# A fused attention and two-layer-block kernel on one core: four tiles together through block 1, and attention 1.5 pairs ahead

## The chip, the cores and the metric

The kernel runs on one core of one Trainium2 chip. The metric is the device time of one execution in microseconds (us). Lower is better. TensorE is called PE here, VectorE DVE, ScalarE ACT, GpSimd POOL, and SP is the queue that issues most DMAs.

## The reference

```python
# attention: q (1, 12288, 128), kv (1, 384, 32, 128), pooled 4 x 4 -> 768 keys
kv_flat = kv_pool.reshape(B, -1, C) @ w_sr          # k = v = kv_flat
s = scale * (q @ k.transpose(0, 2, 1))
a = np.exp(s - s.max(-1, keepdims=True)); a /= a.sum(-1, keepdims=True) + 1e-09
x = a @ v                                           # (12288, 128)
# block 1 (w_in, w_out: 128 x 2048, 2048 x 128)
h = x @ w_in;  g = h * (1.0 / (1.0 + np.exp(-1.702 * h)));  x = g @ w_out
# block 2, weights of its own
h = x @ w_in;  g = h * np.clip(h + 3.0, 0.0, 6.0) / 6.0;    return g @ w_out
```

All inputs are fp32, except that the weights of both blocks are float64 and must be turned into fp32 pairs on the chip.

## The kernel before

**Tiles and units.** The 12288 rows are 24 tiles `t` of 512. Every product is made of three fp32r matmuls: an operand is split into a high part (a copy on ACT, `act_hi`, L118) and a low part (the difference, on DVE, `dve_lo`, L121), and high times low, high times high and low times high are added up in PSUM. A block is cut into eight units per tile, `(m, t, j)`, each of 256 columns of the hidden layer. A unit's first half is `unit_mm` (six matmuls of 512 columns into the PSUM tile `h`, which has two buffers), then the activation, the split of its result into `gh` (ACT) and `gl` (DVE), and `unit_out` (six matmuls of 512 columns into `acc`). In block 1 the activation is a gelu on ACT (L347); in block 2 a relu on ACT (L351) and `unit_swish`, one pass on DVE (L355).

**The main loop** runs over steps `s` (L491). Step `s` issues `unit_mm(s)`, then `unit_out(s - 3)`, then whatever a table `beside` has for (step, "mm"); after that the list `ORDER[m]` gives the order in which ACT's, DVE's and POOL's work of the step is issued. Every engine takes its instructions strictly in that order. Before, the units run by pairs of tiles: 16 steps of block 1, then 16 steps of block 2, so 32 steps a pair and 384 in all.

**Attention beside it.** For each tile there are four subtiles `i`. `s_mm` (L209) makes scores, `s_max` (DVE), `s_exp` (ACT, with the sums as a side output) and `s_norm` (two tiny DVE operations and a scaling on POOL, L234) follow. `t_mm` (L242) transposes the exponentials on PE, `t_hi` and `t_lo` split them. `av_mm` (L267, 18 matmuls, in two halves) multiplies by the values, and `av_end` splits the result into the block's input `x1`. Scores and transposes in the loop share one PSUM tile, `st`, that has a single buffer: the next user must wait until the exp, or `t_lo`, of the last one has read it. `plan_scores` and `plan_values` put these into `beside` by the step numbers in `S_STEPS`, `T_STEPS` and `AV_STEPS`; before, a pair's 32 steps hold the values of the next pair and the scores of the pair after that.

**Weights.** A block's weights are 8 pieces of 512 columns, 16 in all. `w_bits` (six DVE operations) turns the words of a float64 piece into fp32 parts, `w_hi` (ACT) and `w_lo` (two DVE operations) split them. Six pieces are converted in the loop over `kv` ahead of everything (`W_EARLY`), the other ten beside the steps of `W_STEPS`.

**Ahead of the main loop** stand the pooling of `kv` (L446) and a list `FIRST` of pieces for the attention of tiles 0 to 3: `S`core, `T`ranspose, `A` (values), `Q` (split of q), `v`, `W` (a conversion's end), with the stages of each piece issued by `FIRST_STAGES` (stage, how many pieces later).

Of the kernel before, what the change touches and what calls it, by code (L numbers as in the profile page):

```python
# [11 lines left out]
F32 = mybir.dt.float32  # L12
# [6 lines left out]
P = 128  # L19
# [8 lines left out]

T_STEPS = (0, 2, 4, 6, 10, 12, 13, 15)
T_STEPS_0 = (3, 4, 5, 6, 10, 12, 13, 15)
AV_STEPS = (8, 17)
S_STEPS = (16, 18, 20, 22, 24, 26, 28, 30)

ORDER = {
    1: "t_hi gelu w_hi hi_last hi max exp t_lo lo_last lo rest norm end w_lo w_bits".split(),
    2: "max t_hi t_lo relu swish w_hi hi_last exp lo_last norm end rest w_lo w_bits".split(),
}


FIRST = (
    "W S00 S01 S02 S03 v T00 S10 T01 S11 T02 S12 T03 S13 Q2 A0 T10 S20 T11 S21 T12 S22 T13 Q3 "
    "S23 S30 S31 S32 S33"
).split()

FIRST_STAGES = (
    ("t_hi", 0), ("max", 0), ("exp", 1), ("av_end", 0), ("norm", 2), ("w_lo", 0), ("t_lo", 0),
)
A1_STEP = 1  # L50


W_LOADS = {0: "g", 2: "g", 4: "g", 6: "r", 8: "r", 10: "ws"}
W_EARLY = (1, 3, 5, 7, 9, 11)
W_PLACES = "- - - r r ws r r ws r r ws - - ws -".split()
W_STEPS = (0, 2, 3, 5, 7, 9, 11, 13, 16, 18)
POOL_LO = (19, 22)


UPPER_MIN = float(np.uint32(896 << 20).view(np.float32))  # L60
# [4 lines left out]
def tile_pooled_attention__moe_gelu__moe_hardswish(  # L65
# [45 lines left out]
    def f(ap):  # L111
        return ap.bitcast(F32)
# [38 lines left out]
    def w_load(tag):  # L151
        w, src, cs = w_todo.pop(0)
        s = work.tile([P, WL, 2], U32, tag=tag, name="ws", bufs={"g": 3, "r": 2, "ws": 1}[tag])
        nc.sync.dma_start(out=s, in_=src[:, cs, :])
        w_ready.append((w, s, cs))

    def w_bits():

        w, ws, cs = w_ready.pop(0)
        upper = ws[:, :, 1]
        a = work.tile([P, WL], U32, tag="o", name="wa")
        b = work.tile([P, WL], U32, tag="wb", name="wb")
        nc.vector.tensor_scalar(
            out=a, in0=upper, scalar1=0x7FFFFFFF, scalar2=None, op0=ALU.bitwise_and
        )
        nc.vector.tensor_scalar(
            out=f(a), in0=f(a), scalar1=UPPER_MIN, scalar2=UPPER_MAX, op0=ALU.max, op1=ALU.min
        )  # L170
        nc.vector.tensor_scalar(
            out=b, in0=a, scalar1=3, scalar2=0x3FFFFFFF,
            op0=ALU.logical_shift_left, op1=ALU.bitwise_and,
        )
        nc.vector.scalar_tensor_tensor(  # L175
            out=a, in0=upper, scalar=0xC0000000, in1=b, op0=ALU.bitwise_and, op1=ALU.bitwise_or
        )
        nc.vector.tensor_scalar(
            out=b, in0=a, scalar1=0xFF800000, scalar2=None, op0=ALU.bitwise_and
        )  # L180
        nc.vector.scalar_tensor_tensor(
            out=f(b), in0=ws[:, :, 0], scalar=2.0 ** -52, in1=f(b), op0=ALU.mult, op1=ALU.mult
        )
        w_half.append((w, cs, a, b))
        place = w_places.pop(0)
        if place != "-":
            w_load(place)

    def w_hi():
        w, cs, a, _ = w_half[0]  # L190
        act_hi(w[0][:, cs], f(a))

    def w_lo():

        w, cs, a, c = w_half.pop(0)
        dve_lo(f(a), f(a), w[0][:, cs])
        nc.vector.tensor_tensor(out=w[1][:, cs], in0=f(a), in1=f(c), op=ALU.add)

# [22 lines left out]
    def s_exp(t, i):  # L221
        ps, nm = ps_s.pop((t, i)), e_t[t, i]
        e = e_t[t, i] = work.tile([P, NK], F32, tag="e", name="e", bufs=8)
        z = sums_t[t, i] = tiny.tile([P, 1], F32, tag="sums", name="sums")
        nc.scalar.activation(
            e.rearrange("p (b k) -> p b k", b=2), ps[:, :, :h], AF.Exp, bias=nm, accum_out=z
        )

    def s_norm(t, i):
        e, z = e_t[t, i], sums_t.pop((t, i))  # L230
        rec = tiny.tile([P, 1], F32, tag="rec", name="rec")
        nc.vector.tensor_scalar(out=rec, in0=z, scalar1=EPS, scalar2=None, op0=ALU.add)
        nc.vector.reciprocal(out=rec, in_=rec)
        nc.gpsimd.tensor_scalar(  # L234
            out=e, in0=e, scalar1=rec, scalar2=1.0, op0=ALU.mult, op1=ALU.mult
        )

    def t_mm(t, i, *tag):
        e = e_t.pop((t, i))
# [32 lines left out]
    def av_end(t):  # L272
        x1[t] = split_acc(av_acc.pop(t), "x1")

    def split_acc(acc, tag):
        hi = work.tile([P, TT], F32R, tag=tag + "h", name=tag + "h")
        lo = work.tile([P, TT], F32R, tag=tag + "l", name=tag + "l")
        act_hi(hi, acc)
        dve_lo(lo, acc, hi)
        return hi, lo  # L280


    units = []
    for k in range(0, NT, 2):
        for m in (1, 2):
            for t in (k, k + 1):
                units += [(m, t, j) for j in range(NU)]


# [9 lines left out]
    def plan_scores(t, steps):  # L299
        at(steps[0] - 3, "rest", split_q, t)  # L300
        for i, step in enumerate(steps):
            at(step, "mm", s_mm, t, i)
            at(step + 1, "max", s_max, t, i)
            at(step + 1, "exp", s_exp, t, i)
            at(step + 1, "norm", s_norm, t, i)

    def plan_values(t, t_steps, av_step):
        for i, step in enumerate(t_steps):
            at(step, "mm", t_mm, t, i)
            at(step + 1, "t_hi", t_hi, t, i)  # L310
            at(step + 1, "t_lo", t_lo, t, i)
        for k in range(2):
            at(av_step + k, "mm", av_mm, t, range(k * KC // 2, (k + 1) * KC // 2))
        at(av_step + 1, "rest", av_end, t)

    for k in range(2, NT, 2):
        s0 = 2 * (k - 2) * NU
        ts = [s0 + x for x in (T_STEPS_0 if k == 2 else T_STEPS)]
        plan_values(k, ts[:SUB], s0 + AV_STEPS[0])
        plan_values(k + 1, ts[SUB:], s0 + AV_STEPS[1])  # L320
        if k + 2 < NT:
            ss = [s0 + x for x in S_STEPS]
            plan_scores(k + 2, ss[:SUB])
            plan_scores(k + 3, ss[SUB:])
    for s in W_STEPS:
        at(s, "w_bits", w_bits)
        at(s + 1, "w_hi", w_hi)
        at(s + 1, "w_lo", w_lo)
    for k in range(2):
        at(A1_STEP + k, "mm", av_mm, 1, range(k * KC // 2, (k + 1) * KC // 2))  # L330
    at(A1_STEP + 1, "rest", av_end, 1)

    h_t, r_t, g_t, gs_t, acc_t = {}, {}, {}, {}, {}

# [29 lines left out]

    def unit_lo(u):
        gh, gl = gs_t[u]
        (pool_lo if u in POOL_LO else dve_lo)(gl, g_t.pop(u), gh)

    def unit_out(u):
        m, t, j = units[u]  # L370
# [11 lines left out]
    def unit_end(u):  # L382
        m, t, j = units[u]
        if j < NU - 1:
            return
        acc = acc_t.pop((m, t))
        if m == 1:
            x2[t] = split_acc(acc, "x2")
        else:
            o = work.tile([P, TT], F32, tag="o", name="o")  # L390
            nc.scalar.activation(o, acc, AF.Copy, scale=1.0 / 6.0)
            nc.sync.dma_start(out=outT[:, t * TT:(t + 1) * TT], in_=o)

    with tc.manual_schedule():
# [38 lines left out]
        for g_ in range(n_g):  # L433
            pk = big(*slots[g_])[:, 0, :kg]
            cs = slice(g_ * kg, (g_ + 1) * kg)
            for w_ in range(n_w):
                i = g_ * n_w + w_
                if i in (4, 10):
                    split_q(i // 10)
                if i in W_EARLY:  # L440
                    w_bits()
                    w_hi()
                    if i < W_EARLY[-1]:
                        w_lo()
                for w in range(kw // kg):
                    nc.tensor.matmul(  # L446
                        pk, wsr_sb, kvs[i][:, w * kg:(w + 1) * kg],
                        start=(w_ == 0 and w == 0), stop=(w_ == n_w - 1 and w == kw // kg - 1),
                    )
                if w_ == 3 and g_ > 0:  # L450
                    v_group(g_ - 1)
            nc.scalar.activation(k_h[:, cs], pk, AF.Copy, scale=scale / (R * R))
            nc.vector.scalar_tensor_tensor(
                out=k_l[:, cs], in0=pk, scalar=scale / (R * R), in1=f(k_h[:, cs]),
                op0=ALU.mult, op1=ALU.subtract,
            )
            kf[g_] = work.tile([P, kg], F32, tag="x2" + "hhl"[g_], name="kf")
            nc.scalar.activation(kf[g_], pk, AF.Copy, scale=1.0 / (R * R))


        def piece(kind, t=0, i=0):
# [2 lines left out]
                slots.append(slots.pop(0))  # L464
            if kind == "S":
                s_mm(t, i, *slots[-1])
                return {"max": (s_max, t, i), "exp": (s_exp, t, i), "norm": (s_norm, t, i)}
            if kind == "T":
                t_mm(t, i, *slots[-1])
                return {"t_hi": (t_hi, t, i), "t_lo": (t_lo, t, i)}  # L470
# [1 line left out]
                av_mm(t, range(KC))  # L472
                return {"av_end": (av_end, t)}
            if kind == "W":
                return {"w_lo": (w_lo,)}
            if kind == "Q":
                split_q(t)
            else:
# [10 lines left out]

        nu = len(units)  # L490
        for s in range(nu + LAG):  # L491
            if s < nu:
                unit_mm(s)
            if s >= LAG:
# [59 lines left out]
```

## Time and profile before

| | |
|---|---|
| median of 3 runs | 1394.12 us (1393.7 to 1396.24) |
| the profiled execution, its own time | 1396.09 us |
| its span, first to last instruction | 1394.3 us |
| PE busy | 1353.2 us (97%), 6294 matmuls |
| DVE busy | 986.3 us (71%) |
| ACT busy | 1012.3 us (73%) |
| POOL busy | 129.5 us (9%) |
| mean granted clock of PE | 0.990 |

The profiled execution's time is 1.8 us above its span, and 2.0 us above the median. Busy shares are means over the whole span; the page also has the span in 40 slices, where PE shows 7, 8, 6, 8, 8, 9, 9 tenths in the first seven slices (34.9 us each) and 9 or more in all that follow but the last.

### The profile page before, as it was taken

What the parts mean: (1) busy time and instruction counts of PE and PEld (TensorE: products, weight loads), DVE (VectorE), ACT (ScalarE), POOL (GpSimd) and SP (SyncE); (2) the same over time, 40 slices, a digit from 0 to 9 for tenths busy, and PEclk for the clock granted to TensorE, in tenths of its full rate; (3) what the DMA queues carried; (4) which work ended last, traced back from release to release, by engine and by line L of the source; (5) the groups of instructions that cost most, each with busy time, mean ns of one, the idle gap of its engine ahead of it and who ended that gap; (6) DMA issues with size and microseconds to landing.
All of it is one profiled execution on the core that took longest, in us unless ns stands there. A gap on an engine that the chain in (4) does not pass through costs nothing.

```text
span 1394.3 us, 16502 instructions
## 1 busy us (share of the span) xinstructions
PE 1353.2 (97%) x6294; PEld 1132.9 (81%) x6294; DVE 986.3 (71%) x1140; ACT 1012.3 (73%) x1199; POOL 129.5 (9%) x128
## 2 busy tenths in 40 slices
PE   7868899999999999999999999999999999999998
PEld 5756788888888888888888888888888888888887
DVE  7678995686587577478578568568568658757667
ACT  2556678778678678768768777777877877866776
POOL 1310030010010010011011011001001001000000
PEclk9989999999999999999999999999999999999999
DMA  8011000000000000000000000000000000000000
GB/s 326 24 53 46 24 16 8 8 16 8 9 16 8 8 8 16 8 9 16 0 8 16 8 8 16 8 8 16 8 8 16 9 8 8 8 1 8 8 1 16
DMA packets 11167, 28.38 MB, mean 20 GB/s; under 512 B 1232, under 2 KB 1360, under 8 KB 11088
## 3 DMA queue, kind: packets, MB, share of 16 engines
q1 hardware_dynamic: 10944, 27.27, 5.6%
q8 instruction: 49, 0.80, 0.2%
q14 instruction: 30, 0.25, 0.1%
q10 hardware_dynamic: 144, 0.07, 0.0%
HBM read 21.04 MB, written 6.29 MB: 20 GB/s over the span
## 4 chain that ended last, share of the span: by engine, by line
PE 91%; DVE 5%; ACT 2%; issue 1%; DMA 0%; POOL 0%; ACTq 0%; POOLq 0%; DVEq 0%
PE h L343 12%; PE h L342 12%; PE h L341 12%; PE acc L380 12%; PE acc L378 12%; PE acc L379 12%; PE acc L267 6%; PE st L209 6%; PE st L242 4%; PE h L446 1%; DVE gl L121 1%; DVE wa L175 1%; DVE nm L216 1%; ACT gh L118 1%; PE h L209 1%
## 5 line engine op out<-in xcount | busy, mean ns | idle before, releaser
L121 DVE TENSOR_TENSOR gl<-g,gh 128x1024 fp32r<-128x1024 f32 x382 | 472.1, 1238 | 270.4 <-ACT gh L118 270.3
L118 ACT ACTIVATE gh<-g 128x1024 fp32r<-128x1024 f32 x384 | 404.9, 1057 | 26.7 <-PE acc L379 24.0
L351 ACT ACTIVATE r<-h 128x1024 f32<-128x1024 f32 x192 | 197.4, 1028 | 181.6 <-PE h L343 181.6
L380 PE MATMUL acc<-gl,wo_h 128*128 128x512 f32 x768 | 300.2, 391 | 0.4 <-DVE gl L121 0.4
L378 PE MATMUL acc<-gh,wo_l 128*128 128x512 f32 x768 | 300.1, 391 | 0.0
L379 PE MATMUL acc<-gh,wo_h 128*128 128x512 f32 x768 | 299.7, 390 | 0.0
L355 DVE SCALAR_TENSOR_TENSOR g<-r,h 128x1024 f32<-128x1024 f32 x192 | 234.1, 1219 | 91.9 <-ACT r L351 86.2
L347 ACT ACTIVATE g<-h 128x1024 f32<-128x1024 f32 x192 | 197.0, 1026 | 79.1 <-PE h L343 79.0
L380 PEld LDWEIGHTS acc<-gl,wo_h 128*128 128x128 f32 x768 | 144.4, 188 | 32.0 <-DVE gl L121 0.8
L379 PEld LDWEIGHTS acc<-gh,wo_h 128*128 128x128 f32 x768 | 144.5, 188 | 31.9
L378 PEld LDWEIGHTS acc<-gh,wo_l 128*128 128x128 f32 x768 | 144.6, 188 | 30.9
L341 PE MATMUL h<-x1h,wi_l 128*128 128x512 f32 x384 | 158.3, 412 | 0.0
L343 PE MATMUL h<-x1l,wi_h 128*128 128x512 f32 x384 | 151.4, 394 | 0.0
L342 PE MATMUL h<-x1h,wi_h 128*128 128x512 f32 x384 | 151.0, 393 | 0.0
L341 PE MATMUL h<-x2h,wi_l 128*128 128x512 f32 x384 | 150.5, 392 | 0.4 <-DVE g L355 0.4
L343 PE MATMUL h<-x2l,wi_h 128*128 128x512 f32 x384 | 150.8, 393 | 0.0
L342 PE MATMUL h<-x2h,wi_h 128*128 128x512 f32 x384 | 150.4, 392 | 0.0
L234 POOL TENSOR_SCALAR e<-e,rec 128x768 f32<-128x768 f32 x96 | 87.9, 917 | 576.2 <-ACT r L351 246.5
L242 PE MATMUL st<-ident,e 128*128 128x128 f32 x540 | 75.6, 277 | 19.2 <-DVE eTl L121 18.5
L242 PEld LDWEIGHTS st<-ident,e 128*128 128x128 f32 x540 | 65.0, 142 | 32.4 <-issue 11.7
L121 DVE TENSOR_TENSOR eTl<-st,eTh 128x768 fp32r<-128x768 f32 x90 | 85.7, 952 | 1.0 <-ACT eTh L118 0.9
L343 PEld LDWEIGHTS h<-x1l,wi_h 128*128 128x128 f32 x384 | 72.7, 189 | 16.1
(79 smaller groups left out, 1440.9 us busy)
## 6 DMA issues: line engine op xcount, KB each, us to landing
kvs<-kvT SPq DMA_DIRECT2D x12, 512.0 KB, 9.7
q_f<-qT SPq DMA_DIRECT2D x24, 256.0 KB, 2.6
outT<-o SPq DMA_DIRECT2D x24, 256.0 KB, 2.0
ws<-w_in SPq DMA_DIRECT2D x8, 512.0 KB, 4.6
ws<-w_out SPq DMA_DIRECT2D x8, 512.0 KB, 3.8
wsr_sb<-w_sr ACTq DMA_DIRECT2D x1, 64.0 KB, 4.6
```

What stands on the lines that cost most here:

```text
L118: nc.scalar.activation(hi, x, AF.Copy)
L121: nc.vector.tensor_tensor(out=lo, in0=x, in1=f(hi), op=ALU.subtract)
L242: nc.tensor.transpose(pt[:, c // 4, c % 4 * P:(c % 4 + 1) * P], e[:, c * P:(c + 1) * P], ident)
L341: nc.tensor.matmul(hp[:, c, :], wi[m][1][:, ch], xh, start=True, stop=False)
L342: nc.tensor.matmul(hp[:, c, :], wi[m][0][:, ch], xh, start=False, stop=False)
L343: nc.tensor.matmul(hp[:, c, :], wi[m][0][:, ch], xl, start=False, stop=True)
L347: nc.scalar.activation(g, h_t.pop(u), AF.Gelu_apprx_sigmoid)
L351: nc.scalar.activation(r, h_t[u], AF.Relu, bias=3.0)
L355: nc.vector.scalar_tensor_tensor(out=g, in0=r_t.pop(u), scalar=6.0, in1=h_t.pop(u), op0=ALU.min, op1=ALU.mult)
L378: nc.tensor.matmul(acc, wo[m][1][:, ch], gh[:, c, :], start=first, stop=False)
L379: nc.tensor.matmul(acc, wo[m][0][:, ch], gh[:, c, :], start=False, stop=False)
L380: nc.tensor.matmul(acc, wo[m][0][:, ch], gl[:, c, :], start=False, stop=last)
```

## The change

1. The first four tiles form one group: 32 steps of block 1, then 32 steps of block 2. Pairs follow as before.
2. The ten conversions in the loop stand at steps 0, 3, 6, ..., 27 in place of 0, 2, 3, 5, ..., 18. `w_bits` keeps four DVE operations, `w_lo` gets the other two and so has four, one step later. One conversion of the `kv` loop moves, whole, into `FIRST` behind `Q2`. The loads of weights are issued from `w_lo`.
3. The order of a step changes: in block 1, `t_lo` comes second, and `w_hi` behind `hi`; in block 2 conversions fall out.
4. In the pair of tiles `k` and `k + 1`, values are now made for `k + 1` and `k + 2` (before: `k + 2` and `k + 3`) and scores for `k + 3` and `k + 4` (before: `k + 4` and `k + 5`). Transposes in steps of block 1 are issued ahead of the step's `unit_mm` (place "first"), and split in the same step; those in block 2 stay behind `unit_out` and are split one step later. `T_STEPS` and `AV_STEPS` change, `S_STEPS` keeps its numbers.
5. The normalization of a tile's four subtiles is done at once, after the fourth. Two `gl` of early units go from POOL back to DVE. `x2` of tiles 2 and 3 borrows the buffers of weights.

```diff
-T_STEPS = (0, 2, 4, 6, 10, 12, 13, 15)
-T_STEPS_0 = (3, 4, 5, 6, 10, 12, 13, 15)
-AV_STEPS = (8, 17)
-S_STEPS = (16, 18, 20, 22, 24, 26, 28, 30)
+FOUR = 4
+T_STEPS = (0, 2, 4, 5), (8, 10, 12, 14)
+AV_STEPS = (6, 6), (15, 16)
+S_STEPS = (16, 18, 20, 22), (24, 26, 28, 30)
+T_STEPS_0 = {2: (4, 5, 7, 8), 3: (14, 16, 18, 20), 4: (47, 49, 51, 53)}
+AV_STEPS_0 = {1: (1, 2), 2: (11, 12), 3: (21, 22), 4: (55, 56)}
+S_STEPS_0 = {4: (32, 34, 36, 38), 5: (40, 42, 44, 46), 6: (56, 58, 60, 62)}
-    1: "t_hi gelu w_hi hi_last hi max exp t_lo lo_last lo rest norm end w_lo w_bits".split(),
-    2: "max t_hi t_lo relu swish w_hi hi_last exp lo_last norm end rest w_lo w_bits".split(),
+    1: "t_hi t_lo gelu hi_last hi w_hi lo_last lo rest end w_lo w_bits".split(),
+    2: "max t_hi t_lo relu swish hi_last exp lo_last norm end rest".split(),
-    "W S00 S01 S02 S03 v T00 S10 T01 S11 T02 S12 T03 S13 Q2 A0 T10 S20 T11 S21 T12 S22 T13 Q3 "
+    "S00 S01 S02 S03 v T00 S10 T01 S11 T02 S12 T03 S13 Q2 W A0 T10 S20 T11 S21 T12 S22 T13 Q3 "
-    ("t_hi", 0), ("max", 0), ("exp", 1), ("av_end", 0), ("norm", 2), ("w_lo", 0), ("t_lo", 0),
+    ("t_hi", 0), ("max", 0), ("exp", 1), ("w_hi", 1), ("w_lo", 1), ("av_end", 0), ("norm", 2),
+    ("t_lo", 0), ("w_bits", 0),
-W_EARLY = (1, 3, 5, 7, 9, 11)
-W_STEPS = (0, 2, 3, 5, 7, 9, 11, 13, 16, 18)
-POOL_LO = (19, 22)
+W_EARLY = (1, 3, 5, 7, 9)
+W_STEPS = (0, 3, 6, 9, 12, 15, 18, 21, 24, 27)
...
-    def s_norm(t, i):
+    def s_norm(t, i, n=1):
+        if n == 0:
+            return
+        parts = range(i + 1 - n, i + 1)
...
+        for r, p in enumerate(parts):
+            e = e_t[t, p]
+            nc.gpsimd.tensor_scalar(
+                out=e, in0=e, scalar1=rec[:, r:r + 1], scalar2=1.0, op0=ALU.mult, op1=ALU.mult
+            )
...
-    for k in range(0, NT, 2):
+    for tiles in [range(FOUR)] + [(k, k + 1) for k in range(FOUR, NT, 2)]:
         for m in (1, 2):
-            for t in (k, k + 1):
+            for t in tiles:
                 units += [(m, t, j) for j in range(NU)]
...
+    def plan_values(t, t_steps, av_steps):
         for i, step in enumerate(t_steps):
-            at(step, "mm", t_mm, t, i)
-            at(step + 1, "t_hi", t_hi, t, i)
-            at(step + 1, "t_lo", t_lo, t, i)
...
+            late = units[step][0] == 2
+            at(step, "mm" if late else "first", t_mm, t, i)
+            at(step + late, "t_hi", t_hi, t, i)
+            at(step + late, "t_lo", t_lo, t, i)
...
+    for k in range(FOUR, NT, 2):
+        s0 = 2 * k * NU
+        for i in range(2):
+            if k + 1 + i < NT:
+                plan_values(k + 1 + i, [s0 + x for x in T_STEPS[i]], [s0 + x for x in AV_STEPS[i]])
+            if k + 3 + i < NT:
+                plan_scores(k + 3 + i, [s0 + x for x in S_STEPS[i]])
...
         for s in range(nu + LAG):
+            run(s, "first")
             if s < nu:
                 unit_mm(s)
```

## Rows read from the trace of the kernel before

**Rows 1.** Windows, late stretch: busy us of each engine (instructions), PEclk, DMA share, GB/s
```profile
326.00:382.00 56.00, 56.00 (x270) 46.59 (x269) 32.62 (x31) 42.85 (x47) 1.81 (x1) 1.00 0.03 11
```

**Rows 2.** Timeline of PE, late stretch: start us, us, engine, line, operation, tiles [idle before <-releaser]
```profile
316.09 0.51 PE L209 MATMUL st<-k_h,q_h 128*128 128x384 f32 x2
319.91 0.39 PE L341 MATMUL h<-x1h,wi_l 128*128 128x512 f32 x1
322.64 0.81 PE L242 MATMUL st<-ident,e 128*128 128x128 f32 x6
...
328.79 0.82 PE L242 MATMUL st<-ident,e 128*128 128x128 f32 x6
...
376.97 0.40 PE L341 MATMUL h<-x2h,wi_l 128*128 128x512 f32 x1
```

**Rows 3.** Timeline of PE, steps 0 to 32
```profile
73.10 0.50 PE L341 MATMUL h<-x1h,wi_l 128*128 128x512 f32 x1
...
98.37 1.54 PE L242 MATMUL st<-ident,e 128*128 128x128 f32 x6 [10.61 <-DVE eTl L121]
...
110.58 1.51 PE L242 MATMUL st<-ident,e 128*128 128x128 f32 x6 [2.97 <-DVE eTl L121]
...
142.37 1.51 PE L242 MATMUL st<-ident,e 128*128 128x128 f32 x6 [4.59 <-DVE eTl L121]
...
147.50 0.39 PE L378 MATMUL acc<-gh,wo_l 128*128 128x512 f32 x1
...
172.88 0.62 PE L209 MATMUL st<-k_h,q_h 128*128 128x384 f32 x2 [1.20 <-ACT e L225]
...
210.22 0.39 PE L341 MATMUL h<-x1h,wi_l 128*128 128x512 f32 x1
```

**Rows 4.** Timeline of DVE, steps 0 to 14
```profile
78.94 1.23 DVE L121 TENSOR_TENSOR gl<-g,gh 128x1024 fp32r<-128x1024 f32 x1 [2.91 <-ACT gh L118]
...
88.01 0.42 DVE L165 TENSOR_SCALAR wa<-ws 128x512 uint32<-128x512 uint32 x1
...
90.11 0.43 DVE L178 TENSOR_SCALAR wb<-wa 128x512 uint32<-128x512 uint32 x1
...
91.72 1.22 DVE L121 TENSOR_TENSOR gl<-g,gh 128x1024 fp32r<-128x1024 f32 x1 [0.45 <-ACT gh L118]
92.86 0.69 DVE L121 TENSOR_TENSOR wa<-wa,wo_h 128x512 f32<-128x512 f32 x1
...
94.19 0.42 DVE L165 TENSOR_SCALAR wa<-ws 128x512 uint32<-128x512 uint32 x1
...
97.37 0.95 DVE L121 TENSOR_TENSOR eTl<-st,eTh 128x768 fp32r<-128x768 f32 x1
...
142.14 2.28 DVE L121 TENSOR_TENSOR gl<-g,gh 128x1024 fp32r<-128x1024 f32 x1
```

**Rows 5.** Timeline of ACT, late stretch
```profile
321.45 0.20 ACT L225 ACTIVATION_READ_ACCUMULATOR e<-st,nm 128x1 f32 x1
...
350.85 1.03 ACT L347 ACTIVATE g<-h 128x1024 f32<-128x1024 f32 x1 [2.51 <-PE h L343]
352.04 1.06 ACT L118 ACTIVATE gh<-g 128x1024 fp32r<-128x1024 f32 x1 [0.16 <-PE acc L379]
...
380.56 1.28 ACT L225 ACT_TABLE_LOAD   x1
...
382.66 0.19 ACT L225 ACTIVATION_READ_ACCUMULATOR e<-st,nm 128x1 f32 x1
```

**Rows 6.** Timeline of all engines, 30 to 36 us, and of DVE at 58 us
```profile
30.57 1.63 DVE L197 TENSOR_TENSOR wo_l<-wa,wb 128x512 fp32r<-128x512 f32 x1
...
35.46 0.69 PE L209 MATMUL h<-k_h,q_h 128*128 128x384 f32 x1 [5.63 <-ACT k_h L452]
...
35.64 0.41 DVE L453 SCALAR_TENSOR_TENSOR k_l<-st,k_h 128x256 fp32r<-128x256 f32 x1
...
58.03 0.69 DVE L121 TENSOR_TENSOR x1l<-acc,x1h 128x512 fp32r<-128x512 f32 x1 [3.03 <-ACT x1h L118]
```

More of the change, by code (lines that the diff above doesn't have):

```diff
@@ L47 @@
 FIRST_STAGES = (
-    ("t_hi", 0), ("max", 0), ("exp", 1), ("av_end", 0), ("norm", 2), ("w_lo", 0), ("t_lo", 0),
+    ("t_hi", 0), ("max", 0), ("exp", 1), ("w_hi", 1), ("w_lo", 1), ("av_end", 0), ("norm", 2),
+    ("t_lo", 0), ("w_bits", 0),
 )
-A1_STEP = 1
 W_LOADS = {0: "g", 2: "g", 4: "g", 6: "r", 8: "r", 10: "ws"}
-W_EARLY = (1, 3, 5, 7, 9, 11)
-W_PLACES = "- - - r r ws r r ws r r ws - - ws -".split()
-W_STEPS = (0, 2, 3, 5, 7, 9, 11, 13, 16, 18)
-POOL_LO = (19, 22)
+W_EARLY = (1, 3, 5, 7, 9)
+W_PLACES = "- - - r r ws r r ws r r - r r - -".split()
+W_STEPS = (0, 3, 6, 9, 12, 15, 18, 21, 24, 27)
 UPPER_MIN = float(np.uint32(896 << 20).view(np.float32))
@@ L177, in w_bits, with w_hi, w_lo @@
         )
+        w_half.append((w, ws, cs, a, b))
+    def w_hi():
+        w, _, cs, a, _ = w_half[0]
+        act_hi(w[0][:, cs], f(a))
+    def w_lo():
+        w, ws, cs, a, c = w_half.pop(0)
         nc.vector.tensor_scalar(
-            out=b, in0=a, scalar1=0xFF800000, scalar2=None, op0=ALU.bitwise_and
+            out=c, in0=a, scalar1=0xFF800000, scalar2=None, op0=ALU.bitwise_and
         )
         nc.vector.scalar_tensor_tensor(
-            out=f(b), in0=ws[:, :, 0], scalar=2.0 ** -52, in1=f(b), op0=ALU.mult, op1=ALU.mult
+            out=f(c), in0=ws[:, :, 0], scalar=2.0 ** -52, in1=f(c), op0=ALU.mult, op1=ALU.mult
         )
-        w_half.append((w, cs, a, b))
         place = w_places.pop(0)
@@ L187, in w_bits @@
             w_load(place)
[L189 to L195, printed above, removed]
         dve_lo(f(a), f(a), w[0][:, cs])
@@ L223, in s_exp @@
         e = e_t[t, i] = work.tile([P, NK], F32, tag="e", name="e", bufs=8)
-        z = sums_t[t, i] = tiny.tile([P, 1], F32, tag="sums", name="sums")
+        if i == 0:
+            sums_t[t] = tiny.tile([P, SUB], F32, tag="sums", name="sums")
+        z = sums_t[t][:, i:i + 1]
         nc.scalar.activation(
@@ L227, in s_exp @@
         )
-    def s_norm(t, i):
-        e, z = e_t[t, i], sums_t.pop((t, i))
-        rec = tiny.tile([P, 1], F32, tag="rec", name="rec")
+    def s_norm(t, i, n=1):
+        if n == 0:
+            return
+        parts = range(i + 1 - n, i + 1)
+        z = sums_t[t][:, parts[0]:i + 1]
+        rec = tiny.tile([P, n], F32, tag="rec", name="rec")
         nc.vector.tensor_scalar(out=rec, in0=z, scalar1=EPS, scalar2=None, op0=ALU.add)
         nc.vector.reciprocal(out=rec, in_=rec)
-        nc.gpsimd.tensor_scalar(
-            out=e, in0=e, scalar1=rec, scalar2=1.0, op0=ALU.mult, op1=ALU.mult
-        )
+        for r, p in enumerate(parts):
[3 more added lines that the diff above has]
+            )
     def t_mm(t, i, *tag):
@@ L273, in av_end, with split_acc @@
         x1[t] = split_acc(av_acc.pop(t), "x1")
-    def split_acc(acc, tag):
-        hi = work.tile([P, TT], F32R, tag=tag + "h", name=tag + "h")
-        lo = work.tile([P, TT], F32R, tag=tag + "l", name=tag + "l")
+    def split_acc(acc, tag, place=None):
+        if place == "ws":
+            both = work.tile([P, 2, TT], F32R, tag="ws", name=tag, bufs=1)
+            hi, lo = both[:, 0, :], both[:, 1, :]
+        else:
+            hi, lo = (
+                work.tile([P, TT], F32R, tag=place or tag + s, name=tag + s) for s in "hl"
+            )
         act_hi(hi, acc)
@@ L304, in plan_scores @@
             at(step + 1, "exp", s_exp, t, i)
-            at(step + 1, "norm", s_norm, t, i)
-    def plan_values(t, t_steps, av_step):
+            if i == SUB - 1:
+                at(step + 1, "norm", s_norm, t, i, SUB)
+    def plan_values(t, t_steps, av_steps):
         for i, step in enumerate(t_steps):
-            at(step, "mm", t_mm, t, i)
-            at(step + 1, "t_hi", t_hi, t, i)
-            at(step + 1, "t_lo", t_lo, t, i)
[L312 to L324, printed above, removed]
+            late = units[step][0] == 2
+            at(step, "mm" if late else "first", t_mm, t, i)
+            at(step + late, "t_hi", t_hi, t, i)
+            at(step + late, "t_lo", t_lo, t, i)
+        for k, step in enumerate(av_steps):
+            at(step, "mm", av_mm, t, range(k * KC // 2, (k + 1) * KC // 2))
+        at(av_steps[-1], "rest", av_end, t)
+    for t, steps in AV_STEPS_0.items():
+        plan_values(t, T_STEPS_0.get(t, ()), steps)
+    for t, steps in S_STEPS_0.items():
+        plan_scores(t, steps)
+    for k in range(FOUR, NT, 2):
[5 more added lines that the diff above has]
+                plan_scores(k + 3 + i, [s0 + x for x in S_STEPS[i]])
     for s in W_STEPS:
@@ L328, in tile_pooled_attention__moe_gelu__moe_hardswish @@
         at(s + 1, "w_lo", w_lo)
-    for k in range(2):
-        at(A1_STEP + k, "mm", av_mm, 1, range(k * KC // 2, (k + 1) * KC // 2))
-    at(A1_STEP + 1, "rest", av_end, 1)
     h_t, r_t, g_t, gs_t, acc_t = {}, {}, {}, {}, {}
@@ L366, in unit_lo @@
         gh, gl = gs_t[u]
-        (pool_lo if u in POOL_LO else dve_lo)(gl, g_t.pop(u), gh)
+        dve_lo(gl, g_t.pop(u), gh)
     def unit_out(u):
@@ L387, in unit_end @@
         if m == 1:
-            x2[t] = split_acc(acc, "x2")
+            x2[t] = split_acc(acc, "x2", {2: "ws", 3: "wb"}.get(t))
         else:
@@ L442, in tile_pooled_attention__moe_gelu__moe_hardswish @@
                     w_hi()
-                    if i < W_EARLY[-1]:
-                        w_lo()
+                    w_lo()
                 for w in range(kw // kg):
@@ L466, in piece @@
                 s_mm(t, i, *slots[-1])
-                return {"max": (s_max, t, i), "exp": (s_exp, t, i), "norm": (s_norm, t, i)}
+                return {"max": (s_max, t, i), "exp": (s_exp, t, i), "norm": (s_norm, t, i, 1 if t < 2 else i // 3 * SUB)}
             if kind == "T":
@@ L474, in piece @@
             if kind == "W":
-                return {"w_lo": (w_lo,)}
+                return {"w_bits": (w_bits,), "w_hi": (w_hi,), "w_lo": (w_lo,)}
             if kind == "Q":
```

## The prediction

> **What bounds the kernel now.** I read the windows first. In a late stretch of 56 us PE is busy for all 56, at the full clock, while DVE and ACT have a fifth or more of it free [rows 1]. So nothing can be won there, and any new wait of PE is paid in full. PE's timeline gives the prices of the work: a step of twelve matmuls with nothing beside it takes 319.91 to 322.64 = 2.73 us (0.2275 a matmul); two steps and one transposed subtile take 322.64 to 328.79 = 6.15, so a transpose costs 0.69; scores (316.09 to 319.91, less a step) cost 1.09; the 18 matmuls of a tile's values 18 x 0.2275 = 4.10 [rows 2].
>
> The first 32 steps are another matter. They run from 73.10 to 210.22, 137.1 us [rows 3]. Their PE work is 192 + 174 matmuls of the units (83.3), eight transposes (5.5), three tiles of values (12.3) and eight scores (8.7): 109.8. So 27.3 us are lost, and the rows name what ends the waits: DVE's `eTl`, the low half of the transposed subtile before [rows 3]. After a wait PE also runs at half clock, 1.2 of 2.4 GHz: from 142.37 to 147.50 a transpose takes 1.51 in place of 0.81 [rows 2, 3]. DVE is late because it converts weights. A conversion takes, from DVE's starts, 2.10 for four operations, 1.61 - 0.45 = 1.16 for the next two, 1.33 for the last two: 4.59; a `gl` 1.14, an `eTl` 0.87 to the next start and 0.95 in itself [rows 4].
>
> **Four tiles in block 1.** The 32 steps now hold 32 `gl` (36.5), ten conversions (45.9), eight `eTl` (7.0) and six splits of half a `gl`'s size (some 3.5): 93 us of DVE. Before, they held 16 `swish` of a `gl`'s size and eight maxima of an `eTl`'s size more: 18 + 7 more, so 118. PE's work is 109.8 less the eight scores: 101.1. DVE is no longer the longer sum. What remains is local. Followed by hand from `gl` at 78.94: DVE has `gl` 0, four operations, `gl` 1, four operations of 2.49, `gl` 2, a split, `gl` 3, four operations of the second conversion: 11.85, so `eTl` of tile 2's first subtile runs from 90.8 to 91.75 [rows 4]. Its second transpose now stands first in step 5. PE gets there at 73.10, plus steps 0 to 3 without the first three `unit_out` (10.92 - 4.10), the values of tile 1 (4.10), a transpose (0.69) and step 4 (2.73): 87.45 [rows 2, 3]. PE waits **4.2**, rounding off the gaps. A wait of 2.97 and one of 4.59 were each followed by half clock; the second lasted 5.1 us, which cost 2.6, and for the first I take half of that: **2.0** for this one [rows 3]. The fourth transpose (step 8) follows the third by one step, with the conversion of step 6 between them on DVE. `gl` 6 ends some 4.8 after the start of step 6 (1.36 of matmuls, 1.2 from the gelu's start to the copy's, 1.06 of copy, 1.14 of `gl` [rows 4, 5]); with 2.10 and 0.95 that is 7.85, and PE is there after 2.73 + 0.69 + 2.73 = 6.15: **1.7**. At step 11 the values of tile 2 take the `acc` that `x2` of tile 0 frees; its copy now stands behind `w_hi`, which waits for the conversion: **0.7** by the same count, 0 to 1.5. Tile 3's transposes are two steps apart (6.15, or 8.9 from a conversion) and find `eTl` done. Sum **8.6**, against 27.3 lost before: **-18.7**. Bounds: 6.4 if the clock stays up and the last wait is none; 14 if every wait brings half clock of 2.6 and DVE slips by one conversion's half.
>
> **The transpose that stands first.** This is the price of "1.5 pairs ahead". `st` has one buffer. A pair's last scores are in its step 30, and their exp in step 31, behind relu and copy, which wait for that step's own matmuls. In the late stretch the reading of the sums ends at 321.45 + 0.20 = 321.65 [rows 5], and PE starts the next pair's step 0 at 319.91 [rows 2]. Before, the transpose came after that step's twelve matmuls, at 322.64, when `st` had been free for 1.0. Now it comes at 319.91 and must wait until 321.70 (0.05 allowed for the release): **1.79**, with everything of PE behind it. Nothing before it moves: `S_STEPS` and the order relu, copy, exp stand. It meets the pairs that follow scores in step 30, nine of ten (the last has none), and once more inside the four, where a transpose at step 47 stands behind scores at 46, at the same distance (there after twelve matmuls, 2.73, with the exp 4.5 after the step's start): ten times, **+17.9**. Queued behind the waiting transpose is all of PE; behind its split on ACT stand the table load and the gelu of step 0, now some 1.5 later. They do not make PE late again: gelu and copy take some 2.1 of a step's 2.73 [rows 2, 5], so ACT gains 0.6 a step, and `unit_out` of step 0 is three steps off. The row that speaks for no clock penalty is the wait of 1.20, after which the scores went on at full clock [rows 3]; 2.97 is on the other side. 1.79 is nearer to 1.20. If it fell, each would cost another 1.4 to 2.6.
>
> **The values that move away from step 17.** Before, halves of the values stood in steps 17 and 18; now in 15 and 16. The first exp of a block 2 needs a new function table: load 380.56 to 381.84, sums read at 382.85, 5.88 after step 17's first matmul at 376.97 [rows 2, 5]. The next scores are due two steps after it, 5.46, where the values gave 4.1 more. So **0.45** a time (5.93 - 5.46), nine pairs and once in the four: **+4.5**. Bounds 0 and 5.
>
> The Trainium skill speaks against this place (ScalarE: Activation LUTs, What ACT_TABLE_LOAD costs): a switch is about 1283 ns of load and about 1380 ns of drain. The load agrees with the row; by the page's sum the scores would wait 1.83 in place of 0.45 and the total would be higher by ten times 1.38, 13.8. In the row the exp and the reading of its sums are over 1.01 after the load's end, which leaves no place for such a drain.
>
> **Ahead of the loop.** The sixth conversion leaves the `kv` loop. DVE ended the fifth at 30.57 + 1.63 = 32.2; then ACT's copy of the sixth stood ahead of the copies of `k`, PE waited 5.63 until 35.46, and `k_l` ended at 36.05 [rows 6]. Now `v_l` and `k_l`, about 0.4 each, end at 33.0: 3.1 earlier, and up to 5 if PE then keeps its full clock. Against that the conversion's 4.59 come back between tile 0's values, where DVE had 3.03 idle [rows 6], and can start only after the last reciprocal there: 1.6 to 4.6 lost, 2.4 taken. Net **-1.8**, between +1.5 and -3.4. Fewer reciprocals and one pair of table loads less are off PE's path: nothing.
>
> **Edits at nothing.** Work back to DVE from POOL (two `gl`), POOL's four scalings in a row and the borrowed buffers lie where DVE has 23 us of 56 free [rows 1]. The longest `gl` of the early steps took 2.28 in place of 1.23 [rows 4]; even two like it after each row of scalings, 2.1 us, fit into the three steps (8.2) that lie between a `unit_mm` and its `unit_out`, of which matmuls, ACT and `gl` need 4.8. Should that cover go, it is 2.1 a tile. Loads of weights go out one step later, on SP, but pieces were there steps ahead.
>
> **Sum.** -18.7 + 17.9 + 4.5 - 1.8 = **+1.9** on the profiled execution's 1396.1 (span 1394.3 and 1.8 outside), so 1398.0; the median of the runs lies 2.0 lower, 1394.1, and gives **1396.0**. This kernel's measurement tells some 0.2%, 2.8 us, from no change.
>
> **Rivals.**
> *Clock.* The clock falls at each wait of 1.79. At 1.4 to 2.6 each, ten times: 14 to 26 more, 1410 to 1422. It decides from one half of the ten on. For it: 2.97 was enough; against: 1.20 was not. Chance 0.12.
> *No wait at the pair's start.* Then -18.7 - 1.8 and a part of the 4.5: 1374 to 1378. It would need the exp to come 1.8 earlier; that it waits for step 31's relu speaks against. Chance 0.08.
> *DVE still too long* in the first 28 steps: its 93 against 101.1 leave little, and with each conversion a third late the loss is 14 or more: 1401 to 1405. Chance 0.12.
> *A better start*: ahead of the loop -3.4, the first steps 6.4, no wait for the table: 1388 to 1391. Chance 0.11.
> *The table's drain*, as the page has it: 1409. Chance 0.02.
>
> **From cases to numbers.** My forecast, 0.55, is 1396, in its own range 1391 to 1401; of it I give 0.06 faster, 0.32 same, 0.17 slower. Faster: 0.06 + 0.08 + 0.11, less 0.01 = 0.24. Same: 0.32 + 0.01 + 0.02 from the third = 0.35. Slower: 0.17 + 0.12 + 0.10 + 0.02 = 0.41. The range leaves out the clock rival and the absent wait, 0.20 together: 1385 to 1409.
>
> **What would show it.** Right: PE waits of about 1.6 to 1.8 on ACT's exp at each pair's first transpose, 0.3 to 0.5 on the same at the second scores; in the first steps one wait of some 4 on `eTl`, and none of 10. Wrong: PE busy throughout the late stretch, or PE's clock under 1.00 at the pairs' starts, or waits for `gl`.

## The result, and the profile after

The changed kernel takes 1405.45 us (median of 4 runs, 1404.25 to 1405.79), the kernel before 1394.34 (4 runs): a ratio of 1.0076 with a 95% interval of 1.0058 to 1.0093. It is slower by 11 us. The forecast was 1396, with a range of 1385 to 1409 and the largest of its three chances, 0.41, on slower. The profiled execution's span is 1404.0 us, 9.7 longer than before.

The page's head and slices of the changed kernel:

```profile
span 1404.0 us, 16412 instructions
PE 1354.8 (96%) x6294; PEld 1128.0 (80%) x6294; DVE 973.6 (69%) x1010; ACT 1014.7 (72%) x1199; POOL 134.1 (10%) x126
PE   7789999999999999999999999999999999999998
```

PE's work is the same, 6294 matmuls. The third to fifth slices are fuller than before, and yet the whole is longer, so the loss is too thin to show in tenths. Windows show it. The first one below has the bounds of [rows 1]; it holds none of the long waits, only one of 0.29. The second is as long and holds one of the long waits; the third is the 8 us behind another:

```profile
326.00:382.00 56.00, 55.71 (x260) 46.46 (x259) 36.42 (x35) 41.50 (x49) 3.10 (x2) 1.00 0.03 10
400.00:456.00 56.00, 54.23 (x261) 44.78 (x260) 32.71 (x32) 43.42 (x49) 3.56 (x4) 1.00 0.02 6
521.00:529.00 8.00, 7.86 (x41) 6.71 (x42) 4.08 (x6) 6.37 (x8) 3.56 (x4) 1.00 0.00 0
```

The waits of PE over the whole span say what ends the idle time (us in total, times, longest):

```profile
PE st L253 <- issue: 15.7, 10, 1.7
PE st L253 <- DVE eTl L125: 6.4, 2, 4.6
...
PE h L212 <- DVE eTl L125: 4.4, 2, 4.2
PE st L212 <- ACT e L230: 2.9, 10, 0.3
...
PE st L253 <- ACT e L230: 1.6, 1, 1.6
```

The row of 15.7 holds nine waits of 1.68 in the loop and one of 0.59 ahead of it; the last row is the tenth of the same kind, at 296.44.

PE's timeline places the waits. L253 is the transpose (L242 before), L212 the scores (L209), L358 a unit's first matmul (L341):

```profile
59.90 0.61 PE L212 MATMUL h<-k_h,q_h 128*128 128x384 f32 x2 [4.21 <-DVE eTl L125]
...
73.80 0.40 PE L358 MATMUL h<-x1h,wi_l 128*128 128x512 f32 x1
...
92.93 1.51 PE L253 MATMUL st<-ident,e 128*128 128x128 f32 x6 [4.58 <-DVE eTl L125]
...
98.77 0.39 PE L397 MATMUL acc<-gl,wo_h 128*128 128x512 f32 x1
...
107.06 0.85 PE L253 MATMUL st<-ident,e 128*128 128x128 f32 x6 [1.79 <-DVE eTl L125]
...
119.47 0.96 PE L278 MATMUL acc<-eTh,v_l 128*128 128x512 f32 x3 [0.67 <-DVE x2l L125]
...
185.02 0.39 PE L358 MATMUL h<-x2h,wi_l 128*128 128x512 f32 x1
...
239.78 0.85 PE L253 MATMUL st<-ident,e 128*128 128x128 f32 x6 [1.68 <-issue]
...
476.11 0.62 PE L212 MATMUL st<-k_h,q_h 128*128 128x384 f32 x2 [0.29 <-ACT e L230]
...
521.14 0.84 PE L253 MATMUL st<-ident,e 128*128 128x128 f32 x6 [1.68 <-issue]
...
537.12 0.85 PE L253 MATMUL st<-ident,e 128*128 128x128 f32 x6
```

And ACT's, at the same places (compare [rows 5]):

```profile
473.77 1.28 ACT L230 ACT_TABLE_LOAD   x1
475.06 0.90 ACT L230 ACTIVATE e<-st,nm 128x768 f32<-128x768 f32 x1
475.86 0.19 ACT L230 ACTIVATION_READ_ACCUMULATOR e<-st,nm 128x1 f32 x1
...
520.83 0.20 ACT L230 ACTIVATION_READ_ACCUMULATOR e<-st,nm 128x1 f32 x1
```

The first 32 steps run from 73.80 to 185.02, 111.2 us against 137.1 [rows 3]; eight scores, 8.7, have only moved, so 17.2 are won. The wait of 10.6 is gone. From there on each pair gives something back: its 32 steps, from first matmul to first matmul, take 112.37 in place of 109.7 (319.91 - 210.22 [rows 2, 3]). At 521.14 a pair's first transpose starts 0.11 after the sums were read (520.83 + 0.20); the profile calls this releaser "issue" because ACT was just done, but it is the end of the exp, as the row of 1.6 names it. At 476.11 the second scores of a block start 0.06 after the same event behind the table load. The idle times of 1.68 and 0.29 leave out 0.17 of the matmul before, whose end overlaps the next one in an unbroken stream (0.39 long, 0.23 apart): what PE loses is 1.85 and 0.46.

### The profile page after: what moved, and what is told of

The parts are those of the page before. It is cut to its first block, busy times and chain, and to the rows that moved or that the text cites. A ratio compares the mean times of both kernels' runs of the same rounds, so it can differ in the third digit from the quotient of the medians.

```text
span 1404.0 us, 16412 instructions
## 1 busy us (share of the span) xinstructions
PE 1354.8 (96%) x6294; PEld 1128.0 (80%) x6294; DVE 973.6 (69%) x1010; ACT 1014.7 (72%) x1199; POOL 134.1 (10%) x126
## 4 chain that ended last, share of the span: by engine, by line
PE 88%; DVE 4%; ACT 4%; issue 2%; DMA 0%; POOL 0%; SPq 0%; ACTq 0%; DVEq 0%; POOLq 0%
PE h L360 12%; PE h L359 12%; PE h L358 12%; PE acc L397 12%; PE acc L395 12%; PE acc L396 12%; PE st L212 7%; PE acc L278 6%; PE st L253 4%; ACT e L230 1%; ACT gh L122 1%; ACT r L368 1%; DVE gl L125 1%; ACT L230 1%; DVE wa L178 0%
## 5 line engine op out<-in xcount | busy, mean ns | idle before, releaser
L358 PE MATMUL h<-x1h,wi_l 128*128 128x512 f32 x384 | 157.9, 411 | 0.0
L360 PE MATMUL h<-x2l,wi_h 128*128 128x512 f32 x368 | 144.3, 392 | 0.0
L359 PE MATMUL h<-x2h,wi_h 128*128 128x512 f32 x368 | 144.0, 391 | 0.0
L358 PE MATMUL h<-x2h,wi_l 128*128 128x512 f32 x368 | 143.1, 389 | 0.0
L245 POOL TENSOR_SCALAR e<-e,rec 128x768 f32<-128x768 f32 x96 | 96.5, 1024 | 335.6 <-PE st L253 230.6
L128 POOL TENSOR_TENSOR q_l<-q_f,q_h 128x512 fp32r<-128x512 f32 x24 | 36.9, 1537 | 816.7 <-ACT q_h L122 816.7
L253 PE MATMUL st<-ident,e 128*128 128x128 f32 x540 | 74.8, 275 | 24.5 <-issue 15.7
L253 PEld LDWEIGHTS st<-ident,e 128*128 128x128 f32 x540 | 63.0, 141 | 41.9 <-issue 30.8
```

What stands on the lines that cost most here:

```text
L253: nc.tensor.transpose(pt[:, c // 4, c % 4 * P:(c % 4 + 1) * P], e[:, c * P:(c + 1) * P], ident)
L358: nc.tensor.matmul(hp[:, c, :], wi[m][1][:, ch], xh, start=True, stop=False)
L359: nc.tensor.matmul(hp[:, c, :], wi[m][0][:, ch], xh, start=False, stop=False)
L360: nc.tensor.matmul(hp[:, c, :], wi[m][0][:, ch], xl, start=False, stop=True)
```

## The experiments

All runs are against the changed kernel, 1405.4; the kernel before ran beside them at 1393.9 to 1395.1. A difference of about 1 us says nothing: with the same instructions ahead of it, the loop starts between 72.61 and 74.64 in seven profiles (the changed kernel and runs 1, 2, 3, 5, 7 and 9), and the same first 32 steps take 109.99 to 111.22 in five (the changed kernel and runs 1, 2, 3 and 5). The length of one pair, 112.37, repeats within 0.1, so each effect on the pairs is best read there; it is given for the pair that starts at step 128.

**1. Only the first transpose of a pair back behind `unit_out`.**

```diff
-            late = units[step][0] == 2
+            late = units[step][0] == 2 or step % 32 == 0
```

> Only the first transposed subtile of each later pair (step 0 of the pair) goes back behind unit_out and is split one step later; all else as in the changed kernel, 1405.4 us. Theory A (it stands at the head of the step and waits 1.85 us for st, which ACT's exp of step 31 still reads): nine of the ten waits of 1.68 by the profile go, the one at step 47 of the four stays; 1405.4 - 16.7 = 1388.7, between 1387 and 1391. Theory B (the pair's start waits for the normalized exponentials, because all four scalings of a tile now come at once on POOL): the transpose still waits, less than 4 us gained. Theory C (the loss of a pair is spread over many small waits of the new step order): 3 to 8 us gained.

Measured: 1412.08, ratio to before 1.0134 (1.0109 to 1.016). All three theories missed. The wait on the exp is gone, as A said, but the next transpose, still at the head of step 2, now waits for the low half of the first. Waits of PE from 330 to 1300 us, then PE's row and DVE's, of this run:

```profile
PE st L253 <- DVE eTl L125: 19.0, 8, 2.4
```
```profile
527.73 0.85 PE L253 MATMUL st<-ident,e 128*128 128x128 f32 x6 [2.37 <-DVE eTl L125]
```
```profile
526.63 0.95 DVE L125 TENSOR_TENSOR eTl<-st,eTh 128x768 fp32r<-128x768 f32 x1
```

The split of the first was issued a step later, behind a table load, a gelu and two copies on ACT. So 2.37 stands in place of 1.68, 0.69 more, and a pair takes 112.77, 0.40 more; the other 0.28 comes back at the fourth transpose, as the section on the prediction shows. The rest of the rise of 6.6 is the last pair, which had no such wait and now has one of 1.24, and the clock: after one of the nine waits of 2.3 to 2.4 PE ran at half clock for some 3.4 us. The eight us behind two of them:

```profile
1091.00:1099.00 8.00, 7.39 (x39) 6.32 (x40) 3.87 (x4) 5.91 (x7) 0.28 (x1) 1.00 0.10 36
1204.00:1212.00 8.00, 7.36 (x29) 6.02 (x30) 3.89 (x4) 4.75 (x6) 0.32 (x1) 0.79 0.01 2
```

The wait follows the place at the head of a step, not the one transpose.

**2. ACT's exp directly behind max.**

```diff
-    2: "max t_hi t_lo relu swish hi_last exp lo_last norm end rest".split(),
+    2: "max exp t_hi t_lo relu swish hi_last lo_last norm end rest".split(),
```

> Only ACT's order in a step of block 2 changes: exp directly behind max, ahead of relu and the copy. Nothing of PE's order moves. Theory A: the exp then ends some 2.1 us after its scores, before the next step's end, so the waits of 1.85 at the pairs' starts and at step 47 (ten) and of 0.46 behind the table load (ten) all go: 1405.4 - 23 = 1382.5, between 1380 and 1387; relu comes up to 0.5 us later (2 behind a table load), which the three steps before unit_out should hide. Theory B (scalings on POOL): no change, 1404 to 1406. Rival to A: the later relu makes swish and gl late and PE waits for gl in place of the exp: 1390 to 1405.

Measured: 1485.63, ratio 1.0648 (1.0632 to 1.0664). A's number is off by 100 us, and the rival had the right kind and too small a size. Waits of PE from 330 to 1300 us:

```profile
PE h L358 <- DVE g L372: 40.2, 56, 0.9
PE st L253 <- ACT e L230: 19.4, 8, 2.4
```

ACT's timeline of this run:

```profile
503.49 0.90 ACT L230 ACTIVATE e<-st,nm 128x768 f32<-128x768 f32 x1 [2.81 <-DVE nm L219]
504.29 0.19 ACT L230 ACTIVATION_READ_ACCUMULATOR e<-st,nm 128x1 f32 x1
504.38 1.02 ACT L368 ACTIVATE r<-h 128x1024 f32<-128x1024 f32 x1
```

I had overlooked that the exp waits for DVE's max. In front, it stops ACT for 2.81 us, relu and swish come late, and PE waits for a free `h`, which has two buffers, in 56 steps, seven in each pair's sixteen of block 2. A pair takes 120.16. The waits at the pairs' starts did not go either, so the run says nothing for or against the place of the transposes; it shows that the exp's place behind relu, against one directly behind max, is worth 80 us.

**3. The values of a pair's second tile one step later.**

```diff
-AV_STEPS = (6, 6), (15, 16)
+AV_STEPS = (6, 6), (16, 17)
```

> Only the values of a pair's second tile move back by one step, from steps 15 and 16 to 16 and 17, so that 2.04 us of PE work stand between the table load's step and the second scores. Theory A: the wait of 0.46 at the second scores of nine pairs goes, the one in the four stays: 1405.4 - 4.1 = 1401.3, between 1400.5 and 1402.5. Rival: these waits are covered elsewhere (the time comes back as a longer wait at the pair's start): 1405 to 1406.

Measured: 1399.72, ratio 1.0034 (1.0021 to 1.0047). The nine short waits of the pairs are gone and the long ones unchanged (8 of 1.7 from 330 to 1300 us). The gain is 5.7 where 4.1 was expected. A pair takes 111.85, 0.52 less, so nine pairs give 4.7; the loop of this profile also starts 1.2 earlier, which the edit can't cause. The direction holds, and the rival is out.

**4. Normalization one subtile at a time.**

```diff
-            if i == SUB - 1:
-                at(step + 1, "norm", s_norm, t, i, SUB)
+            at(step + 1, "norm", s_norm, t, i, 1)
...
```

The list ahead of the loop is changed in the same way for tiles 2 and 3.

> Only the normalization goes back to one subtile at a time (two tiny DVE operations and one scaling on POOL for each exp). Theory A: off the path, 1404.5 to 1406.5, and the ten waits at the pairs' starts stay at 1.68 by the profile. Theory B (the scalings in a row on POOL delay the transposes or DVE's gl): 1385 to 1395.

Measured: 1404.30, ratio 1.0065 (1.005 to 1.0081), and PE's waits in the late stretch stay:

```profile
PE st L253 <- ACT e L230: 13.0, 8, 1.6
PE st L212 <- ACT e L230: 2.6, 9, 0.3
```

A pair takes 112.36. The four scalings in a row do not matter; theory B is out. That the releaser is now named ACT's exp also confirms how "issue" was read above.

**5. The whole first set of a pair's transposes behind `unit_out`.** The first three are split one step later, the fourth at the end of its own step, since the values follow at once.

```diff
-            at(step, "mm" if late else "first", t_mm, t, i)
-            at(step + late, "t_hi", t_hi, t, i)
-            at(step + late, "t_lo", t_lo, t, i)
+            behind = step >= 64 and step % 32 in (0, 2, 4, 5)
+            last = behind and step % 32 == 5
+            at(step, "mm" if late or behind else "first", t_mm, t, i)
+            after = step + (late or behind and not last)
+            at(after, "rest" if last else "t_hi", t_hi, t, i)
+            at(after, "rest" if last else "t_lo", t_lo, t, i)
```

> All four transposes of a pair's first tile (steps 0, 2, 4, 5) go behind unit_out, the first three split one step later, the last at the end of its own step; the rest as in the changed kernel, 1405.4 us. The run that moved the first one alone lost its wait on the exp but won nothing, because the second, still at the head of step 2, then waited 2.37 us for the low half of the first. Theory A (a place at the head of a step leaves 2.7 us less room, wherever it stands): with all four behind, the 1.85 of nine pairs and the 0.3 of the fourth in ten go and nothing takes their place: 1405.4 - 19.7 = 1385.7, between 1383 and 1389. Rival (ACT, late behind the table load, makes some transpose of the set wait wherever it stands): 1395 to 1412.

Measured: 1385.77, ratio 0.9931 (0.9916 to 0.9946). This is theory A's number to 0.1 us, closer than the spread of the loop's start allows, so that much is chance; a pair takes 110.25, 2.12 less, which is the 1.85 and the 0.28 of the fourth transpose. The sign of the whole change turns: faster than before. From 330 to 1300 us one kind of wait is left:

```profile
PE st L212 <- ACT e L230: 2.6, 9, 0.3
```

**6. The sixth early conversion back in the `kv` loop.**

```diff
-W_EARLY = (1, 3, 5, 7, 9)
+W_EARLY = (1, 3, 5, 7, 9, 11)
...
-S13 Q2 W A0
+S13 Q2 A0
...
```

> Only the sixth early conversion goes back from the list ahead of the loop into the kv loop. By the two traces the main loop starts at 73.80 with the change and at 73.10 without it. Theory A: the 3 to 4 us won at the scores are given back where PE waits 4.2 us at 59.9 for DVE behind the moved conversion, and more: undoing it gives 1404.7, between 1403 and 1406, with the loop's start near 73.1. Rival (the early scores are worth the 1.8 us that I forecast, and the loop's start hides it): 1406.5 to 1409.

Measured: 1404.36, ratio 1.0066 (1.0049 to 1.0083). The main loop starts at 73.10, where it started before the change, in place of 73.80. Both lie inside the spread of 72.61 to 74.64, so the move is worth nothing that can be told, or costs up to about 1 us; the 1.8 us of the forecast are not there.

**7. Tile 2's transposes two steps apart.**

```diff
-T_STEPS_0 = {2: (4, 5, 7, 8), ...
-AV_STEPS_0 = {1: (1, 2), 2: (11, 12), ...
+T_STEPS_0 = {2: (4, 6, 8, 10), ...
+AV_STEPS_0 = {1: (1, 2), 2: (12, 13), ...
```

> Only the transposes of tile 2 move from steps 4, 5, 7, 8 to 4, 6, 8, 10 and its values from 11, 12 to 12, 13. Theory A (two transposes one step apart with a conversion's first half between them on DVE): the waits of 4.58 and 1.79 shrink to some 1.5 and 1.2, the half clock after the first goes, and the 0.67 for x2 goes: 1405.4 - 7 = 1398.4, between 1396 and 1401. Rival (DVE as a whole is too long in the first 28 steps, so the time comes back as waits for gl): 1403 to 1406.

Measured: 1397.94, ratio 1.0024 (1.0015 to 1.0033), a gain of 7.5. PE's rows of this run:

```profile
92.69 0.85 PE L253 MATMUL st<-ident,e 128*128 128x128 f32 x6 [1.90 <-DVE eTl L125]
105.73 0.85 PE L253 MATMUL st<-ident,e 128*128 128x128 f32 x6 [0.59 <-DVE eTl L125]
```

4.58 and 1.79 became 1.90 and 0.59, the wait for `x2` went, and after 1.90 the transpose took 0.85, the full clock's time. The first 32 steps take 103.77. DVE's total is not what binds these steps.

**8. Split of q behind the sixth conversion.**

```diff
-S13 Q2 W A0 T10
+S13 W A0 Q2 T10
```

> Only the order of three pieces ahead of the loop: the split of tile 2's q comes behind the sixth conversion and tile 0's values, not ahead of them, so that POOL's q_l does not run beside the conversion's first operations (which took 1.48 and 1.02 us in place of 0.42 and 0.43 while it ran). Theory: DVE ends the conversion some 1.6 us earlier, PE's wait of 4.21 shrinks by as much, and the loop starts near 72.2 in place of 73.8: 1405.4 - 1.6 = 1403.8, between 1402.5 and 1405. Rival (the wait comes from ACT, whose copy of the conversion stands ahead of x1h): unchanged, 1404.8 to 1406.

Measured: 1404.53, ratio 1.0075 (1.0057 to 1.0093). The loop starts at 73.35, and at 73.48 in run 10; the gain that I expected, 1.6, is not there, and one of 0.3 to 0.5 is not told from none. DVE did end the conversion earlier, but the late q became the wait:

```profile
57.98 1.01 PE L212 MATMUL h<-k_h,q_l 128*128 128x384 f32 x2 [3.03 <-POOL q_l L128]
```

**9. Four repairs together**: the edits of 3, 5 and 7, and tile 4's transposes at 48, 50, 52, 54 (values at 56, 57), so that none follows scores by one step.

> Four repairs in one: the first set of transposes of a pair behind unit_out (-19.7 by theory A), the values of the second tile in steps 16 and 17 (-5.7 as measured), tile 2's transposes two steps apart (-7), and tile 4's transposes one step later, so that none follows scores by one step (-1.85). If they are independent: 1405.4 - 34 = 1371, between 1369 and 1376, against 1394.6 of before. If PE's waits only move from one to the next: 1385 to 1400.

Measured: 1372.87, ratio 0.9839 (0.9824 to 0.9853). They add up, within 2 us. A pair takes 109.71, as before the change. From 330 to 1300 us PE has no wait at all; over the whole span the largest left in the loop is

```profile
PE st L253 <- DVE eTl L125: 2.2, 2, 1.6
```

**10. The same with the later split of q.**

> The four repairs together (1372.9 us) and the later split of q. If the gain ahead of the loop adds to them: 1371.3, between 1370 and 1372.3; if what is ahead of the loop is taken up by DVE's first steps: 1372.5 to 1374.

Measured: 1372.49, ratio 0.9843 (0.9827 to 0.9858), not to be told from run 9.

## Why the prediction was right, and where its sizes were off

The places and the mechanisms of the three large terms were right, and the largest chance lay on slower. That the number fell into the range is partly luck: 1405.45 lies outside 1391 to 1401, which the forecast's own case had, and the part of the range above that came from rivals that did not occur, DVE too long as a whole (1401 to 1405) and the table's drain (1409).

**The transpose that stands first**: right in place, mechanism and size. Ten waits of 1.85 (1.68 by the profile) were forecast as 1.79 each, 17.9 against 18.5. Run 1 alone would have spoken against it; run 5, which removes the place at the head of the step for all four, gave the nine waits back. What failed is "They do not make PE late again". In the changed kernel the fourth transpose, at 537.12, starts 0.14 after the end of the low half of the third. PE's, ACT's and DVE's rows of one pair, and PE's and ACT's of the last pair, whose first transpose finds `st` free:

```profile
533.44 0.82 PE L253 MATMUL st<-ident,e 128*128 128x128 f32 x6
534.01 0.48 PE L358 MATMUL h<-x1h,wi_l 128*128 128x512 f32 x1
537.72 0.48 PE L358 MATMUL h<-x1h,wi_l 128*128 128x512 f32 x1
...
534.76 0.79 ACT L122 ACTIVATE eTh<-st 128x768 fp32r<-128x768 f32 x1
...
536.03 0.95 DVE L125 TENSOR_TENSOR eTl<-st,eTh 128x768 fp32r<-128x768 f32 x1
```
```profile
1313.75 0.81 PE L253 MATMUL st<-ident,e 128*128 128x128 f32 x6
1314.32 0.48 PE L358 MATMUL h<-x1h,wi_l 128*128 128x512 f32 x1
1317.75 0.48 PE L358 MATMUL h<-x1h,wi_l 128*128 128x512 f32 x1
...
1314.74 0.79 ACT L122 ACTIVATE eTh<-st 128x768 fp32r<-128x768 f32 x1
```

The places are the same, yet the step with the fourth transpose takes 3.71 behind a wait and 3.43 without one; a bare step takes 2.72. The rows lay the difference to ACT: it copies the third transpose 1.32 after that one's start behind a wait, and 0.99 after it in the last pair. ACT has no pause from the table load at 523.44 until 536.7, so it has not made up what the wait cost it. The forecast's 0.6 gained in a step left out ACT's copies of the transposes, 0.79 each. In run 1, where the first transpose of a pair does not wait, though its second does, the step takes 3.43 in most pairs too. No run changes ACT alone, so the cause is read from these rows and not tested. It is some 0.28 in each of nine pairs, 2.5 us, a term that was put at nothing.

**The values that move away from step 17**: right. Forecast 0.45 ten times (5.93 - 5.46 is in fact 0.47); measured 0.46 by the idle time and 0.53 by the steps, 4.32 from first matmul to first matmul against 3.79 in run 3, which took it out. Here too the exp starts 0.01 after the load's end (473.77 + 1.28, 475.06), and the load starts 0.02 after the copy ahead of it: no drain is seen. By the sum that the Trainium skill gives for a table switch (ScalarE: Activation LUTs, What ACT_TABLE_LOAD costs) the wait would have been 1.83, an estimate; the measurement decides against it.

**Four tiles in block 1**: forecast -18.7, measured -17.2. The waits were 4.58, 1.79 and 0.67 by the profile against 4.2, 1.7 and 0.7; half clock lasted from 92.93 to near 98.8, so it cost nearer to 2.9 than to 2.0. That is where the 1.5 went. Much of it belongs to this execution: in run 1, with the same instructions, half clock lasts some 3.4 us behind a wait of 4.36 there, which costs 1.7, and the 32 steps take 110.03.

**Ahead of the loop**: the step of the forecast that failed outright, -1.8 against +0.7 between the two profiles (-0.5 to +1.5 over the seven that share the code). The scores did start earlier, as said: at 30.52, and 32.92 for those with `k_l`, in place of 35.46. But "2.4 taken" for the returning conversion was too little: it delayed PE by 4.21 at 59.90, and half clock followed there too. Two rows of DVE of the changed kernel and two of POOL show one part:

```profile
52.15 1.48 DVE L168 TENSOR_SCALAR wa<-ws 128x512 uint32<-128x512 uint32 x1
53.66 1.02 DVE L171 TENSOR_SCALAR wa<-wa 128x512 f32<-128x512 f32 x1
```
```profile
52.05 1.29 POOL L128 TENSOR_TENSOR q_l<-q_f,q_h 128x512 fp32r<-128x512 f32 x1
53.32 1.08 POOL L245 TENSOR_SCALAR e<-e,rec 128x768 f32<-128x768 f32 x1
```

Two operations that take 0.42 and 0.43 in the other conversions took 1.48 and 1.02 while POOL worked, and each ends 0.3 after one of POOL's. The Trainium skill (SBUF — State Buffer, SBUF: two separate sides) describes the port that both share as a lock held for an instruction; that the two rows end behind POOL's agrees. Run 8 moved the first of these meetings away (0.41 in place of 1.48; the second operation still took 1.03, beside a scaling) and won little, because q itself was then late; which part of the 4.21 is the lock's and which the order's stays open.

**The sum.** +0.7 - 17.2 + 18.5 + 5.3 + 2.5 = 9.8, against 9.7 measured between the two spans. The forecast's +1.9 lacked 2.5 of the fourth transposes, 2.5 ahead of the loop, 1.5 in the first steps and 1.4 of the two waits; another 1.4 is that the medians lie 11.1 apart and the spans 9.7. All of these lie on one side, so nothing cancelled; the two largest terms stood.

**The rivals.** The clock did not fall after the waits of 1.85: PEclk is 1.00 in the 8 us behind each of the ten, as in the window 521 to 529. It was not far from it: waits of 2.3 to 2.4 in run 1 were followed by half clock once in nine. DVE was not too long as a whole (run 7). The absent wait, the better start and the table's drain did not occur.

## What to carry to other kernels

A place at the head of a step is not the same as one at its end: an operation that shares a single buffer needs its predecessor's last reader to be done, and moving it forward past the step's twelve matmuls (here 2.7 us) uses up slack that no busy share shows. Before moving one, read when the buffer is really released, in the row of the last reader, for every neighbour in the set, and move or keep the set as a whole; moving one member back made things worse. A change that frees an early stage can be worth keeping once its side effects are repaired one by one: here 1394 became 1405 and then 1373.

## What the runs showed that I had not expected

PE's clock kept its full rate after the ten idle times of 1.63 to 1.68 us in the changed kernel and one of 1.90 in run 7, and fell after 4.58; the rows of before have a fall after 2.97 [rows 3]. In between the same wait can go either way: of run 1's nine of 2.28 to 2.38 one was followed by half clock, at 1204.64, and eight were not. An instruction that waits in order is dear on ACT: the exp set ahead of the relu stopped the engine for 2.81 us at 503.49, and the eight exps of a pair together cost some 8 us.
